# A fifth pair of column blocks in partial sums, a sixth slot for exponentials, and new order tables, in a two-layer attention and token-mixing kernel

## The chip, the core and the metric

The kernel runs on one core of a Trainium2 chip. The metric is the device time of one execution in microseconds. Lower is better. A core has a matrix engine (PE, which the kernel calls tensor), a vector engine (DVE, vector), an activation engine (ACT, scalar), a general engine (POOL, gpsimd) and an engine that issues transfers (SP, sync). Each works through its own list of instructions in order, and they wait for one another through semaphores.

## The reference

Two layers, each an attention half and a token-mixing half. S = 2048 tokens, D = 512, 32 heads of 16, a causal window of W = 256, F = 1792. All inputs are bf16.

```python
def _A_ref(x, wqkv, wo):
    qkv = (x @ wqkv).reshape(B, S, 3, H, Dh).transpose(2, 0, 3, 1, 4)
    q, k, v = qkv[0], qkv[1], qkv[2]
    scores = einsum("bhqd,bhkd->bhqk", q, k) * Dh ** -0.5
    mask = (i - j >= 0) & (i - j < 256)
    p = softmax(where(mask, scores, -1e9))
    o = einsum("bhqk,bhkd->bhqd", p, v)
    return o.transpose(0, 2, 1, 3).reshape(B, S, D) @ wo

def _B_ref(x, w1, b1, w2, b2):
    h = layernorm(x)
    u = gelu(einsum("bsd,sf->bdf", h, w1) + b1)
    return (einsum("bdf,fs->bds", u, w2) + b2).transpose(0, 2, 1)

x = A_x
x = x + _A_ref(layernorm(x), wqkv, wo)
x = x + _B_ref(layernorm(x), w1, b1, w2, b2)
x = x + _A_ref(layernorm(x), wqkv, wo)
x = x + _B_ref(layernorm(x), w1, b1, w2, b2)
```

The second half mixes over tokens: its first product sums over all 2048 tokens, so a value of u needs the normalised input x-hat (`xh_sb`) of every token.

## The kernel before

**How the order comes about.** The program is written as jobs that record operations with what they read and write. A list of jobs is sorted by due time and then visited in the order of a table, `ORDER`. A second table, `BANKS`, gives the PSUM bank (6 or 7) of the helper products. A third, `LINES`, gives the list of each of the five engines outright: which operation stands at which place, and for copies, masks and normalisations that more than one engine can do, on which of them it stands. These tables are packed strings. The semaphores follow from the recorded reads and writes. All large transfers are issued by SP, so a transfer that waits holds back those behind it in SP's list.

**Attention.** Each layer works on 4 groups Q of 512 queries, 4 head tiles t of 8 heads, and 9 steps m, so 144 steps. A step has scores on PE (L795, in cells of 64x64, into one of two halves of four PSUM banks), an exponential on ACT (L806, into slot n % NSLOT of `p_sb`), a mask on DVE or POOL (L823), and PV on PE (L844, banks 4 and 5). After m = 8 the sums are copied out to `oU` and `o2` (L440 on DVE, L442 on ACT, which are the two ends of one helper, `copy_out`), and transfers collect denominators (den_c<-oU) and the rest (oU<-o). Between the steps PE does the projections of q (L591), k (L622) and v (L695), transposes (L567, L580), the normalise product (L887) and the product with wo (L760). The layer norm has statistics (L525, L526) on DVE and small operations on POOL, and is applied (xh_sb) on ACT (L547), or by DVE or POOL (L544). L637 is ACT's half of masking k and q, L632 DVE's; L710 and L715 write `v_all`.

**Partial sums.** The 14 blocks of 128 columns of w1 are handled in 7 pairs. For the first PART = 8 blocks, `job_part` sums over chunks 0 to 7 (tokens 0 to 1023) while attention still works on the later tokens. It reads the lower weights from `w1low`, which holds two pairs, and uses 64 matmuls of 64x64 cells for a pair (L607). The sums go to `ubuf` as fp32 (`acc_at`).

**The MLP.** `job_u` computes u block by block, the whole blocks first, then the part blocks. A whole block has four groups of 4 matmuls of 128x128 by 128x512 (L983), a part block has the last two groups, and DVE adds the partial sum (L988). ACT applies gelu (L990). The upper weights of the part pairs lie in `xhT` (pairs 0 and 1) and `k_sb` (pairs 2 and 3), the weights of the three whole pairs in the three slices of `w1buf`; the third slice is loaded once for both layers. `job_y` multiplies by w2 (L1029). w2's homes are `w1buf[0]`, `w1buf[1]` and the two halves of `oU`. In layer 0 the tiles 8 to 15 of y are computed inside layer 1's attention, in cells (L607 too); the last tile of layer 1 is done in halves (L1017). The sum with the residual is on DVE (L1033, L1006, L1021).

**Hand-overs.** There are three. From attention to the MLP: after the last PV come the normalise product, wo, two layer norms, and x-hat of tokens 1536 to 2047 (tiles 12 to 15), and PE fills the time with u groups that need only the earlier tiles. From layer 0 to layer 1: after the first eight tiles of y come the layer norm of the first tokens, transposes, and k, q and v of the first group. Inside attention: every second head tile ends with the copies and transfers named above.

Of the kernel before, what the change touches and what calls it, by code (L numbers as in the profile page):

```python
# [10 lines left out]
P = 128  # L11
# [5 lines left out]
PART = 8  # L17
# [12 lines left out]
def _table(*text):  # L30
# [5 lines left out]
    'c-pm-Ne;ju3<DYe|It<36QUtoiNu9qWIOQ~ckvvCUEkdu!hhkTGe1YTP~@rQU0fFp^)x;4x-$AF=Njp%un%%{$-(R<s119<{N!Zp&wOBPJZ2gw'  # L36
    '_#DUKdY*TM)IMraJ>OSnL0d(ACotVqnr}=Y&BW*Olgl)%J+933^`8{tWL?s+0Cx')
ORDER = _table(
    'c-jTQ17Hvc00q#G>{_;$ZQEM5ZQHnPo6ELs+qP}qdjKJXM+g|95E5aK5^)h0kr5i<5E0Q40Z|YM(U1_a5EU^I196Z5fry9Lh>v7Qj6}$YBuIgz'
    'NQ2}^g|x_l)JTU+$d86dkF3ao?8uB_$c1dkgPh2K0OUh%6ht}XMPU>`Q4~TE)I~{@MsZX{36w=CR74q+M<wh-5UQXlDx*58p%yxzChDLDx}gGU'  # L40
    'qdpp=I~t%KnxPR|U?TdWC7Pf$nxidRp$*!jGlrlO+My%5peuS}9@e8bMxh7#qZbCD9|mGHrei1uU^up+4+di-{=*22#TbmoZVbZ&Ou;xD!emUt'
    'RLsO|%)%VZ#SARKB+SPmEJQGt;sh3BIhJ81R^cqxVhuK6HP&GXHen;SVg){9Gqzv{wqqB*;4=1OC-&k14&pwJ;4qHiDQ@5tj^YeX;yCu;JWk^r'
    'F5(jI;R3EAB(LBauHz4G;}-7VChp=P9^eVy;5i=S5uV{CUg0&~;sqk{15)!nKH?odAt}G(D}Lh}e&Hv`4EzBw1pgrnO))gXGXk?R3L`T*OEQ45'
    '7@N^pkx?0!aTt*aS%V1}pNW}_F&K`Cn1m@9ipiOZe-X%(OvAKH$Mg)#{EWve%*f2l#9WNY?99fT%)=ba&AiOVRxHQ@EW*NU$YLDDLM+PSEWu7J'
    '%~CAOaxB9N3}Sg!VI|gLW!7X}R%dNCU>(+DBQ|DzR%J6bXHzy|OSWKJwr3l5VLNtaNA_TEc4K$;Vm}UGPj+Qr4&p!#<zNnDAO6RYoX9a8!PXqd'
    '(HzV1oWRMP!v37eX`IU0oWWU~$N8MZxm?60T*$>-%3!YGYA)wWuHrhb<$7-CHE!TlZsc_i;R5dAGG5^(?&frE;Z5G=X0G8a-rx>y<xXznF7D+%'
    'p5y`U=P4fMSsv$69^?fc;|ZST5uW2Ap5aBF=Oy0ZWj^LzKHz;m;ypg(dp_fHzTi`S<P*N+8@}Z$zUDiA;3t0JAAaR`M$<Qb<}ZfV4~EcB{w4K~'
    'zZpjs6iQM^g;p3vRX9adVue*?MNlN=RSX3vtD-2n;wh$LDYfD%ff6acnkcCfD!Gy<nF3W#sZ>)Ll}<&JM(LGZnbl93ludb*LpfDnxm8g4)k#y8'
    'PlZ)L#Z*W=)LNxgROMAll~h(0RasS3O+yr0HB?o#Rb91IR}EE1jnzQS)JRR$LM@d`DV0H4lveH3M$HwZR_dU(YOgZttZwR}3hJto>aG&%rM~K|'
    '0qUc{>aRf>rjDwo5gMxD8m)mErLh{L@tUC7nxtu3pk<n<8JeP5>Z$3PsX3afd77`)TC9aSpkOW4a;?xv?b0f()EceTIIY(@ZPX@h&=zghHf`52'  # L50
    '?a)r`(QfV4WbM--ZPh^?)(IWaQ61N5oz!`q(J5WjSzXX2UDge~*A?B>65Y{l-PAK(*EQYO13l7H-O@RQ@I$@OW4+Z?J<)T$)JMJ1Ywgz;z0(JM'
    ')=z!XJ^j`Xebq1h(>KBLEB#eS({^ZwaeRkzIEQsaf7c&HaU@4@fFnDaqdTUPI)-CAj^jDJqdJx2I*}7Ni4!`pW4Vk2oy;kn+&P`W>73eWT*zIW'
    '!kL`jX`R&>oyB!r#krls&79r2T*P^t*L_^rrCiL#o!R+a!j)Xs*__YiT+!7X<kGI}f-dTkuIXy7=kl)M`mXDSZsaCz>I!b*R&L|gZtsq6;M#8M'
    '4sPx)uIldY?4IuC9`5DdZs*4C?|vTW0dDCb9_GOw>7gFs;U4309__In?+Kpd$?ofEp5m#V=^38o*<R!W-tRfy>p@=XQQqfep6iL8=fghe`JV1W'
    'KH?=_=mlQvV6XCKZ}Cbm_X=<IHt+NvZ}cXw_Xe-=TCesluk#LX_imr`d7tqmAN4U`^>Lr_37_^2pYuhZ^=)79Jzw!P-}hx-_Z{E#1K;&6KlCF%'
    '_7ndP&4=a!')
LINES = {
    "tensor": _table(
    'c-jrshkFRt769;j?>Xn5dv22ojaH4KjVDIZMA1GJv4a>-(HfPg5yYO!vqzMo)>C_ab`ce|pAa>kM6H_PqgIOw5<!T({t>_LS5bwkN~*G|qN=Je'
    '6|O#35h_wORne-Nicu|8JJnjXQD3M&DnTWw8ETZ8ppw;EHD66p^VA}>O6^e#)i$+KZB!f7Nwq^AP+QecYM(l!Zm1*bjC!JutBdM_%2J|ltE=iy'  # L60
    'bxWO4)72yOhssrD^-J}a%2A|Wr~=hk7uE0TNL@+?>Eb#>m((BXP+duf>)tv{SJ$8DT6&`Xr;gI|bzR+3ch?JaU)@5->4Ey9UaNcQ;W|kV(8F}1'
    '9;=gesve^!>uGw9UZ!(&1+z+T)JODEy;7&>4SJhCs_*EZ^?qI5?9gd?pFXHFb%s8p>zVWVy6$GK>EHED{fB<2|J2#~vCh|5^h;f+-)J_@3^0Kv'
    'zyzDpCdrgH<xHpvF<`2iDkjndnJg1wJ~cH>9dq4uG__3=)7f+}TTCzWjp=Lln?+`*8EN{MA;!QsGs28DlgwnZ*~~Gs&3yA8^TaGOOU+8N!E}IB'
    'v%~B$8Rn4LZPLs!bKIOXr%W+8Z_b&E=8|awcg=cuWbT*;Cf~$Cp?P5}6c~a)cpC=6`%nVPL0JfeN^lgyAq?umC8z-npgDMmg2vDaVxS#7Gyj4w'
    ';VbA0U&Azrg#OSQ5+EMNKnRS0p^yZfa3Una1egNJU~v}Agt>4ZR=^xs4y$1el)z1}5q7~r*aBN29kxLVWWshh1Bc-!$bt+w4OihN?0{6b2RGmj'
    'JcPgCH59;8$bnn{RQL>nFb{(9ITXRt_zsrB7Z8Fkp%Q+Cp%{U+u`JfZy4VaGVhaqzcGwXUFb+Fl0QSUK?1Ayv2NN*~Be5EOg4J;<j>8&Q6F<ez'
    'a0ZUWWc&_i<2)RQOK=dbz{R*62jdzXf~#>e4#i=Zg2QnWZo>n(AJgy=9>NiL7;`We8{q=X#&tLmJ)On^e1mUMCceOzn1$ysA8+7AEW{!dK#%bm'
    '22oK`^aS(p6_%zl6iUHVj*3xn3ZxQLiK<c<g-``5Pw!I%MbhWghU!uSYDm%4oZ8Y58cP4B(G*90DS^6EFN&vuG>XR40GdD}X(p|u*|dPNXg;l='
# [274 lines left out]
def bass_interleave_layers__sliding_block__mixer_token_mlp__prompt_kernel(  # L343
# [816 lines left out]
```

## Time and profile before

| | |
|---|---|
| three runs | 504.71, 505.14, 503.58 us (median 504.71) |
| the profiled execution | 504.01 us |
| its span on the core | 502.3 us |
| TensorE clock granted | 0.999 |

The profiled execution's own time is 1.7 us more than its span. The profile page has the busy time of each engine over the span, the chain of work that ended last, and groups of instructions by line. The windows cut the span into stages and give each engine's busy time there. Roughly, layer 0's attention runs from 14 to 164 us, the hand-over to its MLP from 164 to 188, the MLP from there to 230, layer 1's attention from about 232 to 408, and its MLP from there to the end. Three rows of each list of waits give the scale of what the engines waited for (engine, result and line that waited, what it waited for, total, times, longest):

```profile
ACT xh_sb L547 <- POOL shift L541: 34.7, 5, 11.5
...
ACT ubuf L990 <- DVE ps L988: 13.0, 14, 2.0
...
PE ps L591 <- issue: 2.7, 17, 0.2
PE ps L795 <- ACT p_sb L806: 2.3, 6, 0.7
...
PE ps L695 <- ACT wqkv L686: 1.1, 1, 1.1
```

ACT has long waits, since it is little used outside attention. PE's waits are few and short.

### The profile page before, as it was taken

The numbers are of one execution on the slowest core, as the hardware profiler recorded it, in microseconds if no ns is written. First come the engines' busy times: TensorE is split into PE (matmuls) and PEld (weight loads), VectorE is DVE, ScalarE is ACT, GpSimd is POOL, SyncE is SP. The second block draws the span as 40 slices with busy tenths as digits, with TensorE's granted clock in tenths as the row PEclk, the third lists the DMA queues.
The fourth block names the chain that finished last, engine by engine and source line by source line (L and its number), as shares of the span: only waits on it lengthen the run. The fifth ranks groups of instructions, "written<-read, shape, count | busy, mean of one in ns | idle before, by whom it ended". The sixth has DMA issues, their size and how long they took to land.

```text
span 502.3 us, 19381 instructions
## 1 busy us (share of the span) xinstructions
PE 474.3 (94%) x8385; PEld 272.0 (54%) x8454; DVE 323.4 (64%) x660; ACT 315.6 (63%) x381; POOL 213.1 (42%) x375
## 2 busy tenths in 40 slices
PE   8898989998999999998998999999999999999997
PEld 4454556555766444444444776566547754444444
DVE  7989988887663571366897447878886549131222
ACT  2898999997999314400776669889989960340000
POOL 5897756664564030001874555577544312200000
PEclk9999999999999999999999999999999999999999
DMA  6922222242222725050002140114214256050661
GB/s 209 96 79 84 70 71 77 85 114 68 78 62 70 216 79 147 0 147 1 24 9 61 50 137 15 38 61 136 85 47 114 71 156 185 0 146 12 198 200 52
DMA packets 76516, 44.52 MB, mean 89 GB/s; under 512 B 8976, under 2 KB 75408, under 8 KB 76432
## 3 DMA queue, kind: packets, MB, share of 16 engines
q1 hardware_dynamic: 72560, 43.27, 29.3%
q0 software_dynamic: 3872, 0.02, 1.4%
q8 instruction: 66, 1.08, 0.9%
q14 instruction: 18, 0.15, 0.1%
HBM read 32.51 MB, written 2.10 MB: 69 GB/s over the span
## 4 chain that ended last, share of the span: by engine, by line
PE 70%; ACT 8%; DVE 6%; POOL 6%; issue 4%; DMA 3%; SPq 2%; DVEq 0%; ACTq 0%; POOLq 0%
PE ps L1029 14%; PE ps L983 13%; PE ps L795 9%; PE ps L844 8%; ACT p_sb L806 7%; PE ps L591 7%; PE ps L607 7%; PE ps L760 4%; PE ps L695 4%; POOL p_sb L823 3%; SPq L434 2%; PE ps L519 1%; PE ps L887 1%; DMA w1buf<-in_B_w_dram 1%; POOL xh_sb L544 1%
## 5 line engine op out<-in xcount | busy, mean ns | idle before, releaser
L806 ACT ACTIVATE p_sb<-ps 128x1024 bf16<-128x1024 f32 (+8 forms) x288 | 261.5, 977 | 47.4 <-PE ps L795 39.0
L823 POOL TENSOR_TENSOR p_sb<-p_sb,edge 128x128 bf16<-128x128 bf16 (+2 forms) x263 | 127.4, 491 | 114.1 <-ACT p_sb L806 99.3
L795 PE MATMUL ps<-q_sb,k_sb 64*64 64x288 bf16 (+8 forms) x2816 | 108.5, 249 | 3.4 <-ACT p_sb L806 2.3
L844 PE MATMUL ps<-p_sb,v_all 64*34 64x288 bf16 (+17 forms) x2816 | 92.1, 246 | 4.4 <-issue 1.5
L795 PEld LDWEIGHTS ps<-q_sb,k_sb 64*64 64x64 bf16 x2816 | 60.0, 106 | 46.6 <-ACT p_sb L806 22.6
L844 PEld LDWEIGHTS ps<-p_sb,v_all 64*64 64x64 bf16 (+1 forms) x2816 | 60.0, 100 | 21.5 <-POOL p_sb L823 6.3
L591 PE MATMUL ps<-xhT,wqkv 128*128 128x512 bf16 x214 | 55.4, 380 | 4.8 <-issue 2.7
L823 DVE TENSOR_TENSOR p_sb<-p_sb,edge 128x128 bf16<-128x128 bf16 (+2 forms) x137 | 39.9, 300 | 21.9 <-ACT p_sb L806 14.5
L1033 DVE SCALAR_TENSOR_TENSOR x_sb<-ps,b2col,x_sb 128x512 bf16<-128x512 f32 x23 | 17.1, 750 | 44.4 <-PE ps L1029 43.9
L537 POOL TENSOR_TENSOR rstd<-vare,mhalf 128x4 f32<-128x4 f32 (+1 forms) x17 | 16.6, 977 | 67.1 <-DVE vare L535 53.9
L983 PE MATMUL ps<-xh_sb,w1buf 128*128 128x512 bf16 x186 | 44.1, 379 | 0.6 <-issue 0.5
L525 DVE BATCH_NORM_STATS2 stats<-x_sb 128x6 f32<-128x512 bf16 x64 | 43.0, 681 | 0.6
L710 POOL TENSOR_TENSOR v_all<-vt,even 128x1024 bf16<-128x1024 f32 (+2 forms) x23 | 34.3, 1495 | 17.3 <-DVE vt L698 17.3
L547 ACT ACTIVATE xh_sb<-x_sb,shift,rstd 128x512 bf16<-128x512 bf16 x11 | 8.8, 813 | 50.5 <-POOL shift L541 34.7
L632 DVE TENSOR_TENSOR k_sb<-ps,half 128x1024 bf16<-128x1024 f32 (+1 forms) x32 | 37.3, 1166 | 4.7 <-PE ps L622 2.4
L1029 PE MATMUL ps<-ubuf,w1buf 128*128 128x512 bf16 x165 | 37.4, 379 | 0.2
L607 PE MATMUL ps<-xh_sb,w1low 64*64 64x512 bf16 x512 | 35.5, 377 | 0.1
L1029 PE MATMUL ps<-ubuf,oU 128*128 128x512 bf16 x150 | 34.5, 379 | 0.2
L988 DVE TENSOR_TENSOR ps<-ps,ubuf 128x512 f32<-128x512 f32 x16 | 11.2, 700 | 35.1 <-PE ps L983 35.1
L591 PEld LDWEIGHTS ps<-xhT,wqkv 128*128 128x128 bf16 x240 | 19.5, 98 | 26.5 <-issue 4.4
L695 PE MATMUL ps<-xhT,wqkv 128*128 128x512 bf16 x114 | 30.1, 380 | 3.5 <-issue 1.4
L990 ACT ACTIVATE ubuf<-ps,b1col 128x512 bf16<-128x512 f32 x28 | 19.0, 686 | 22.9 <-DVE ps L988 13.0
(89 smaller groups left out, 531.4 us busy)
## 6 DMA issues: line engine op xcount, KB each, us to landing
w1buf<-in_B_w_dram SPq DMA_DIRECT2D x30, 256.0 KB
w1buf<-in_B_w_dram SPq DMA_DIRECT2D x50, 128.0 KB
oU<-in_B_w_dram SPq DMA_DIRECT2D x18, 256.0 KB
oU<-o SPq DMA_DIRECT2D x16, 256.0 KB
w1low<-in_B_w_dram SPq DMA_DIRECT2D x32, 128.0 KB
q_sb<-qt SPq DMA_DIRECT2D x120, 32.0 KB
xhT<-in_B_w_dram SPq DMA_DIRECT2D x4, 512.0 KB
k_sb<-in_B_w_dram SPq DMA_DIRECT2D x4, 512.0 KB
```

Source lines behind the costliest of these rows:

```text
L525: dve(lambda e: e.bn_stats(stats[:, t, :], x_sb[:, t, :]), 690, prio, reads=[R("x", t)], writes=[R("stats", t)])
L591: last = e.matmul(ps[:, b, :], lhsT=wqkv[:, c, c0:c0 + P], rhs=xhT[:, buf, c, :], start=(c == 0), stop=(c == 3))
L607: last = e.matmul(ps[64 * h:64 * h + 64, banks[r ^ swap], :], lhsT=lhs(r ^ swap, c, rows, 64 * h), rhs=rhs(r ^ swap, c, rows), start=(c == ...
L632: return e.tensor_tensor(dst, src.unsqueeze(2).to_broadcast([P, n, 2, w]), mask[:].unsqueeze(1).unsqueeze(3).to_broadcast([P, n, 2, w]), o ...
L695: last = e.matmul(ps[:, b, :], lhsT=wv[:, c], rhs=xhT[:, buf, c, :], start=(c == 0), stop=(c == 3))
L710: return e.tensor_tensor(dst, src.unsqueeze(2).to_broadcast([P, n, 2, DH]), even[:].unsqueeze(1).unsqueeze(3).to_broadcast([P, n, 2, DH]), ...
L795: last = e.matmul(ps[64 * c:64 * c + 64, 2 * half + r, 32 * i0:32 * i1], lhsT=k_sb[rows, ring, t, kb % 16, :], rhs=q_sb[rows, t, c, 32 * i ...
L806: exps[plan.job] = last_exp[0] = plan.op({ACT: (170 + int(2 * (512 - c0) * 0.84), lambda e: e.activation(p_sb[:, slot, :, c0:512], ps[:, 2 ...
L823: return e.tensor_tensor(v, v, g, op=ALU.mult)
L844: last = e.matmul(ps[64 * r:64 * r + w, B_O + (c ^ r), 32 * i0:32 * i1], lhsT=v_all[rows, pos - 32 * c:pos - 32 * c + w], rhs=p_sb[rows, s ...
L983: r = e.matmul(ps[:, b, :], lhsT=blk[:, sc - 8 * part, (ft % 2) * P:(ft % 2 + 1) * P], rhs=xh_sb[:, sc, :], start=(sc == 8 * part), stop=( ...
L1029: r = e.matmul(ps[:, b, :], lhsT=blk[:, turn[n], (st % 2) * P:(st % 2 + 1) * P], rhs=u_at(turn[n]), start=(n == 0), stop=(n == NFT - 1))
```

## The change

PART goes from 8 to 10, so job_part handles five pairs. The third slice of w1buf goes, and an own buffer `w1more` of half its size holds the upper weights of the fifth pair; ubuf grows by two blocks. p_sb has six slots. The due time of the fifth pair's upper load is 60 us into the layer. All three tables are new, so places and engines of many operations are new too, also where nothing else changed.

```diff
@@ -14,7 +14,7 @@
-PART = 8
+PART = 10
@@ -33,91 +33,92 @@
 BANKS = _table(
...
 ORDER = _table(
...
 LINES = {
...
@@ -361,7 +362,7 @@
-    NSLOT = 5
+    NSLOT = 6
@@ -387,7 +388,8 @@
-        w1buf = sb("w1buf", [P, 3, NT, 256])
+        w1buf = sb("w1buf", [P, 2, NT, 256])
+        w1more = sb("w1more", [P, 8, 256])
         w1low = sb("w1low", [P, 2, 8, 256])
         ubuf = sb("ubuf", [P, (NFT + PART) * D])
@@ -927,6 +929,8 @@
             if fb >= NLOW:
                 return w1buf[:, fb - NLOW], [R("w1", fb - NLOW, j) for j in range(8)]
+            if fb == 4:
+                return w1more[:], [R("w1more")]
@@ -1095,7 +1099,7 @@
-                todo.append((base + (76 + 2.5 * k if k < 2 else 100 + 0.1 * k), lambda p, k=k: w1_high_dma(k, p)))
+                todo.append((base + (76 + 2.5 * k if k < 2 else 100 + 0.1 * k if k < 4 else 60), lambda p, k=k: w1_high_dma(k, p)))
```

What the tables change can be counted in the lists of the two programs, operations by engine:

| operation | before | after |
|---|---|---|
| PE L607, cells | 960 | 1088 |
| PE L983, u groups | 320 | 288 |
| DVE L988, adds of partial sums | 16 | 20 |
| ACT copies to o, oU, qt, ubuf | 6, 7, 9, 5 | 9, 8, 10, 6 |
| ACT copies of 128x1024 to xhT | 1 | 3 |
| ACT masks to k_sb, to q_sb | 2, 0 | 4, 2 |
| ACT to v_all, 128x512 | 4 | 2 |
| x-hat on ACT, DVE, POOL | 11, 28, 25 | 12, 32, 20 |
| SP loads to w1buf (w1), w1low, w1more | 50, 32, 0 | 42, 40, 2 |

Of the order three things are named by the prediction. In front of k of layer 1 (L622) there stood 4 matmuls of y after the last transposes, and now there stand 14. The 64 cells matmuls of the fifth pair stand, in both layers, behind the last PV and ahead of the first normalise product. Where layer 0's third query group ends its first pair of head tiles, SP's list held eight transfers from the first of the denominators to oU<-o, and now holds six.

More of the change, by code (lines that the diff above doesn't have):

```diff
@@ L40 @@
[L40 to L44, printed above, removed]
@@ new lines @@
+    ')w*i;r>k&{uEEv0Cig${-bza'),
+    "scalar": _table(
+    'c-jTQYfKho6ae6Jd(V5$`-4@Au|g}<yktwAE*!WTbJMl3BFkp7NiO+8mQ5)gk?4jj$xT?0I`P7~IHqOF`qTv$iB3(oD9kcPsf|Wi>4q*e*7Mv4'
+    'g-`%bz<ely8puEk?11G^1?yoGG(jD-!Zz3sZSW0rLOb+87hHsH7=ZI|3Vwq@_!|_5;BFj-yKp?_;$(aTXJP@qk40FFkK<CTz!mrgc4HN;#X4-n'
+    '9axX8*oL2B20L&ceuZbT7yIxs4&XJsg)b41Qx=V;QItoM=wX^p`81nepi(NQ3R*=!(`u@rT56<bYN0*UPKW4AIzeZshtAOz`h#xLZ6Z#b&G+&+'
+    'p2YcF$kTWZ&*LY#gcoudFXLDEHD1Y8yp}=gxSqH0cK(15a|fT`(|nFE@UPs@H~BwKk|m>LjEt3;GE0i2SW2W+%4C_WmI|qsTG=QKvQ=7Sw;Ys8'
@@ new lines @@
+    'IV9b3NlwdN>5`-JkBkht!NQD?6FA%-ri6bbKMc#bFfmLGvqD*@3~z_#us!SwABJrq6Apxi@I^QlPKGn#`*0zg55I@2;d;o@937!!b&O8bsamK-'
+    'I#-|8=k!%wrE9cWYqVZlb*t{tPxPQ>v{O%Nul}gNXun?7>v}^uj*b)JJ#kumC^qVQnjeee+&H99#l>+!TpG*c`nVx(jGJRq+!@>B-gqQ_9=qc4'
+    'csBOLzIZtf#KDNBmSx#?r{&rMHr|$4fz7aw;uM=_#rCW%wsKo;Z`xb-u5Gq0)?&NuW7}sL>#+TH%8uJH`_6u_KD%PqY|u)5gb&*R&+{CA(5L&O'
+    'KHKN`0$=3i?q1<5y~=C6(VKmzxA`-E#6R_~z0-g4Uhnrye#8IrKYhrD{f?BK^3r4JTc40D<)-=R`Lrfgr<c=`RGD5(@1&;mda6z9QbXF5{s;A3'
+    '$m9'),
+    "gpsimd": _table(
```

142 lines of the change are left out of this document (69 added, 73 removed).

## The prediction

> **What bounds the kernel now.** I read busy times and chain shares first, then the windows by stage, then the waits of TensorE and ScalarE, then chain and timeline where a wait is longer than 0.5 us. Busy times and the shares of the chain that ended last:
>
> ```profile
> PE 474.3 (94%) x8385; PEld 272.0 (54%) x8454; DVE 323.4 (64%) x660; ACT 315.6 (63%) x381; POOL 213.1 (42%) x375
> PE 70%; ACT 8%; DVE 6%; POOL 6%; issue 4%; DMA 3%; SPq 2%; DVEq 0%; ACTq 0%; POOLq 0%
> ```
>
> PE is busy 474.3 of 502.3 us. An edit that leaves its work alone can gain at most the 28 us in which it stands idle. The windows say where those are (columns: stretch, length, busy time of each engine, clock, DMA share, GB/s):
>
> ```profile
> 60.00:112.00 52.00, 48.37 (x1276) 29.92 (x1279) 44.34 (x86) 49.64 (x56) 29.68 (x45) 1.00 0.30 86
> 112.00:164.00 52.00, 48.65 (x1415) 33.15 (x1422) 30.59 (x63) 47.83 (x53) 27.03 (x50) 1.00 0.25 72
> 164.00:188.00 24.00, 23.40 (x183) 10.96 (x186) 16.58 (x36) 5.20 (x9) 4.72 (x8) 1.00 0.51 149
> 188.00:230.00 42.00, 41.79 (x199) 19.16 (x201) 16.56 (x31) 12.74 (x19) 3.69 (x6) 1.00 0.30 88
> 230.00:260.00 30.00, 26.82 (x381) 14.14 (x385) 25.07 (x50) 16.35 (x22) 16.27 (x27) 1.00 0.05 12
> 352.00:408.00 56.00, 53.79 (x1420) 35.96 (x1428) 38.54 (x72) 51.57 (x59) 24.24 (x45) 1.00 0.31 88
> ```
>
> In the MLP (188 to 230) PE idles 0.2 us of 42: only fewer matmuls would help there. In layer 0's attention (60 to 164) PE has 97.0 of 104 us and ACT 97.5: two engines are full at once, ACT with 6.5 us to spare. The hand-over to layer 1 (230 to 260) has PE's largest gap, 3.2 us. What ACT and PE waited for (total, times, longest):
>
> ```profile
> ACT p_sb L806 <- PE ps L795: 39.0, 47, 11.6
> ...
> ACT p_sb L806 <- PE ps L844: 5.5, 8, 1.7
> ...
> PE ps L622 <- DVE xhT L440: 1.8, 1, 1.8
> ...
> PE ps L844 <- DVE o L440: 0.9, 1, 0.9
> ```
>
> The exponentials mostly wait for scores, little for a slot that a PV matmul (L844) frees. PE's two named stalls are single events: k of layer 1, and a PV behind a copy.
>
> **The fifth pair.** The chain prices both kinds of matmul (start, us, line, count):
>
> ```profile
> 151.63 1.73 PE ps L607 x32
> ...
> 183.31 7.77 PE ps L983 x36
> ```
>
> 32 of L607 take 1.73 us (54 ns each, in 64x64 cells), 36 of L983 7.77 (216 ns). The change moves the lower half (chunks 0 to 7) of two column blocks from job_u, 2 x 8 = 16 of L983 per layer (320 to 288 in all), 3.45 us, to job_part, 64 of L607 per layer (960 to 1088), 3.46 us: PE's work is unchanged. Nor does it move to where ACT could cover it. In the changed PE list the 64 stand in both layers behind the last PV, just ahead of the first normalise (L887), where PE is alone and full (164 to 188: 23.4 of 24); only 8 more L607 stand inside an attention, 0.43 us, given back after it. Value 0; if the list ran as an own stage with nothing beside it, it is still 0. What comes with the pair: two DVE adds per layer (L988, 16 to 20, 0.70 each) under PE groups of 0.86 us; uncovered they cost 4 x 0.70 = 2.8, a loss only. Two copies to ubuf per layer (0.59) beside the outproj and normalise matmuls. Four more low-weight loads per layer on SP (w1low 32 to 40) and one of w1more, against eight w1buf loads fewer; the pair's low weights come when the third pair's are read, its upper ones behind the fourth query group's first exponential, a quarter of the attention ahead of the MLP that reads them; eight w2 loads of twice the size took 8.2 us, so four cost about 2 us if nothing hid them, and behind them on SP stand q and oU loads. I take 0: the DMA share in attention is 0.25 to 0.31.
>
> **Hand-over to layer 1.** In front of k (L622) DVE's copies of the transposes come late:
>
> ```profile
> 231.94 0.39 DVE L440 COPY xhT<-ps 128x512 bf16<-128x512 bf16 x1
> ...
> 232.39 1.05 PE L622 MATMUL ps<-xhT,wqkv 128*128 128x256 bf16 x8 [1.84 <-DVE xhT L440]
> ```
>
> Before, one group of y (four L1029, 0.86 us) stands between the last transposes and k. The new list puts 14 L1029 there (14 x 0.216 = 3.0 us), work that had to be done anyway. The 1.84 us stall is covered by 2.2 us more: -1.6, keeping 0.2 for copies shifted by the new order. Bounds -1.84 and 0 (if DVE's copies come later by as much).
>
> **The output copy in layer 0.** At 116 to 122 the den_c and oU loads queue on SP, and PE (0.94) and ACT (0.80, 0.91, 0.92 in its timeline) stall behind them:
>
> ```profile
> 116.77 1.96 DMA den_c<-oU
> ...
> 118.75 2.35 DMA oU<-o
> ```
>
> Before, SP's list holds eight loads from the first denominator to oU<-o, one of which (w1buf) waits for an exponential; the new list holds six, with no such wait among them. Value -0.9, PE's stall; bounds 0 and -2.6 (ACT's three gaps).
>
> **Copies on ACT.** The new lists give ACT, in both attentions, 3 more copies to o (0.61 each), 1 to oU (0.63), 1 of qt (0.60), 1 to ubuf (0.59), 2 large ones to xhT (1.05), and 2 fewer to v_all (0.72): 1.8 + 0.6 + 0.6 + 0.6 + 2.1 - 1.4 = 4.3 us, some 3.6 of it in layer 0. Every one stands ahead of exponentials in ACT's queue, and scores wait for the banks that these free. The chain passes through exponentials for 10.2% of 60 to 112 and 17.3% of 112 to 164, so I take 0.15 x 4.3 = +0.6. Bounds 0 (the spare 6.5 us take them) and +4.3. DVE is relieved by the same copies; it is not full in any of these windows except 60 to 112 (44.3 of 52).
>
> The Trainium skill (ScalarE: Activation LUTs, section What ACT_TABLE_LOAD costs) says that back-to-back activations overlap by about 93 ns. By it each of the six net added copies costs 0.09 less, 0.5 in all, and this term would be 0.15 x 3.8 = +0.6 too. The trace agrees: five exponentials of 1.03 us each took 4.75 us, 0.10 of overlap apiece.
>
> **Six slots.** An exponential may run one step further ahead of the PV that frees its slot. At most this gives back the 5.5 us that ACT waited on L844. But 5.2 of them lie at 240 to 408, where PE is busy 160.1 of 168 us: ACT would wait for PE elsewhere. I take the same 0.15, -0.8; bounds 0 and -5.5.
>
> **Start.** The first v projection (L695) waited 1.1 us on an ACT copy of wqkv; in the new lists it does not, but the first exponential comes only about 0.2 earlier: -0.2, bounds -1.1 and 0.
>
> **From attention to the MLP.** The tiles 12 to 15 of the last group need outproj, LN twice and x-hat before the u groups that read them:
>
> ```profile
> 187.41 1.52 ACT L547 ACTIVATE xh_sb<-x_sb,shift,rstd 128x512 bf16<-128x512 bf16 x2 [8.22 <-POOL shift L541]
> ```
>
> x-hat is done at 188.93; PE reaches the first reader after 7 groups of 0.86 from 183.31, at 189.3. With one more pair in parts only 6 such groups are left in both layers, so PE comes 0.86 earlier; x-hat comes about 0.5 earlier, as two of its four applies go to DVE (two in 1.05 us, against 1.52 on ACT). The margin of 0.4 (in layer 1 x-hat at 431.4, PE at 431.8: the same) goes to about 0. I take 0.2 per layer, as the LN chain may not bring all of the 0.5: +0.4; bounds 0 and +1.7 (one group per layer). The w2 loads behind it took 8.2 us in a burst and have 8 to 12 us before their first reader: 0.
>
> **Sum.** -1.6 - 0.9 + 0.6 - 0.8 - 0.2 + 0.4 = -2.5. The profiled run took 504.01 us, 502.28 of them span; so 501.5 for such a run. The median of the runs shown is 0.7 higher, 504.71, and so 502.2.
>
> **Rivals.**
> 1. Slower: ACT sets the pace of layer 0's attention. The copies count in full, +4.3, and as ACT is then always behind, neither the SP stretch nor the sixth slot gives anything: 504.7 + 4.3 - 1.6 - 0.2 + 0.4 = 507.6. It decides from where some 70% of the 4.3 lie on the path. For it: ACT is busy 97.5 of 104 us. Against: the 6.5 us spare, and ACT's 39 us of waiting on scores. Chance 0.20.
> 2. The hand-over runs dry: normalise and LN finish 1.3 us later per layer, since the pair's copies and stats share DVE with them (adds and stats now stand ahead of the reciprocal in layer 1). 502.2 + 2.6 = 504.8. For it: a margin of 0.4 at 189. Against: PE's pair there, 3.5 us, is cover itself. Chance 0.10.
> 3. Removed waits are taken over by others, the change being a re-sorting of equal work: 504.2 to 504.7. For it: PE 93% and ACT 94% full at once, so what one stall gives the next may take. Against: the stall at 232 has pure PE work behind it. Chance 0.17.
> 4. The pair is hidden after all, PE running closer: 3.45 - 0.43 = 3.0 us per layer off on top of the sum, 502.2 - 6.0 = 496.2. Against: the list puts it where PE is alone and full (23.4 of 24). Chance 0.03. The Trainium skill (Trainium Kernel Development and Optimization, section Performance Expectations) holds that busy matmul time tells little of the distance to the roofline, because matmuls are pipelined, and takes the weight loads' share instead. Here that is 54%, and by this rule PE would have room for rival 4. The rows of the MLP speak against it: 36 matmuls follow one another at 0.216 us with no gap while PEld is at 46%.
>
> **How the numbers follow.** The forecast has 0.50, its own range 499.5 to 503.9: most bounds of the gains on one side, the loss of either large gain on the other. The range reaches to 499.0 and, into rival 1, 507.2. This kernel's measurement can tell about 0.3%, 1.5 us: faster is under 503.2, slower over 506.2. Faster: 0.42 from the forecast, 0.01 each from rivals 2 and 3, 0.03 from 4: 0.47. Same: 0.08 + 0.03 + 0.06 + 0.13 = 0.30. Slower: 0.17 from rival 1, 0.03 each from 2 and 3: 0.23.
>
> **What would show it.** Right: no wait of L622 on xhT over 0.3 us at 232; no PE stall on o near 121; ACT's waits on L844 under 4 us; L607 at 54 ns per instruction in its new place; PE without a gap over 0.3 at the first L983 that reads tile 12. Wrong: ACT over 100 us busy in the first 104 us of full attention with that stage longer (rival 1), a new wait of PE on x-hat or on oT at the MLP's start (rival 2), equal stages with other names among the waits (rival 3).

## The result and the profile after

The changed kernel takes 496.98 us (median of 4 runs, 496.20 to 497.66), the kernel before beside it 504.92 (503.58 to 506.26). The ratio is 0.9842, 95% interval 0.9809 to 0.9875: 7.9 us faster. The forecast was 2.5 us; 496.98 lies below its range. The profiled run took 497.66 us with a span of 495.9 (before 504.01 and 502.3), so the two traces have 6.4 us to explain.

The page of the changed kernel, busy times and the shares of the chain that ended last:

```profile
PE 472.4 (95%) x8478; PEld 272.3 (55%) x8550; DVE 325.5 (66%) x661; ACT 320.6 (65%) x392; POOL 211.4 (43%) x372
PE 78%; DVE 9%; ACT 5%; issue 4%; DMA 2%; SPq 2%; POOL 1%; DVEq 0%; ACTq 0%; POOLq 0%
```

PE has about as much to do as before (474.3) in a shorter span. The chain has moved from ACT (8 to 5%) and POOL (6 to 1%) to PE (70 to 78%) and DVE (6 to 9%). Where the time left is read from the starts of PE's matmuls in the traces, in us; the last column is a second profile of the changed kernel:

| stage | before | changed | changed again |
|---|---|---|---|
| start to the first scores | 14.76 | 15.26 | 13.93 |
| layer 0, first scores to last PV | 150.86 | 148.99 | 149.20 |
| last PV to the first y | 42.71 | 42.33 | 42.34 |
| first y to the first transpose of layer 1 | 20.29 | 20.28 | 20.28 |
| that transpose to the first scores | 10.37 | 8.43 | 8.43 |
| layer 1, first scores to last PV | 169.04 | 165.95 | 165.41 |
| last PV to the first y | 42.74 | 43.12 | 43.14 |

From the first y of layer 1 to the end all three take 51.5. The start differs by 1.3 us between two runs of one kernel, so nothing of it is put down to the change. What remains is three pieces: layer 0's attention 1.7 to 1.9, the way to layer 1's scores 1.9, layer 1's attention 3.1 to 3.6. The split is good to about 1 us: the kernel with the filler in the old lists (below), the same as before in layer 0, shows 149.68 there, and the one with another SP order in layer 0 shows 170.19 in layer 1. The hand-overs to the MLP cancel. Much of the gain lies early in each attention: the first 56 exponentials take 54.7 and 55.3 us in layer 0 (before 56.4), and 65.1 and 64.0 in layer 1 (before 67.4). The windows of the changed kernel (stretch, length, busy time and count of PE, PEld, DVE, ACT, POOL, clock, DMA share, GB/s):

```profile
60.00:112.00 52.00, 48.40 (x1315) 30.59 (x1326) 44.47 (x83) 50.44 (x57) 31.23 (x48) 1.00 0.26 74
112.00:164.00 52.00, 49.17 (x1368) 33.18 (x1370) 30.92 (x59) 48.26 (x54) 28.61 (x54) 1.00 0.30 88
164.00:188.00 24.00, 23.50 (x232) 10.65 (x224) 16.84 (x38) 4.28 (x7) 4.65 (x7) 1.00 0.48 138
188.00:230.00 42.00, 41.79 (x200) 19.03 (x203) 19.08 (x37) 11.48 (x17) 2.11 (x3) 1.00 0.30 88
230.00:260.00 30.00, 29.25 (x438) 16.16 (x444) 27.26 (x52) 22.65 (x34) 16.76 (x33) 1.00 0.08 22
```

ACT is busier than before in the two windows of layer 0's attention (98.7 of 104 us, was 97.5) and the stage is shorter all the same. PE's gap at 230 to 260 has shrunk from 3.2 to 0.75 us. The waits (total, times, longest):

```profile
ACT p_sb L808 <- PE ps L797: 24.8, 41, 2.2
...
ACT p_sb L808 <- PE ps L846: 1.5, 5, 0.4
```

```profile
PE ps L797 <- ACT p_sb L808: 4.3, 7, 1.2
...
PE ps L697 <- ACT wqkv L688: 1.0, 1, 1.0
```

ACT's waits for a slot went from 5.5 to 1.5 us, its waits for scores from 39.0 to 24.8. In exchange PE now waits 4.3 us (2.3 before) for an exponential to free a score bank, and the v projection still waits 1.0 us for wqkv. The timeline of PE at the start of layer 1 in the changed kernel (start, us, operation, count, and in brackets an idle time ahead of it):

```profile
228.61 2.11 PE L1033 MATMUL ps<-ubuf,oU 128*128 128x512 bf16 x9
230.55 0.39 PE L569 MATMUL ps<-ident,xh_sb 128*128 128x128 bf16 x4
230.78 1.03 PE L1033 MATMUL ps<-ubuf,oU 128*128 128x512 bf16 x4
231.64 1.91 PE L624 MATMUL ps<-xhT,wqkv 128*128 128x256 bf16 x16
```

Where PE stood 1.84 us ahead of k, y matmuls now run among and behind the transposes, and k follows without a gap. Between the first transpose and the first scores stand 18 y matmuls, as before the change: then 4 of them stood among the transposes, none behind the last, and 14 between the halves of k and q. Now all 18 stand ahead of k.

### The profile page after: what moved, and what is told of

The parts are those of the page before. It is cut to its first block, busy times and chain, and to the rows that moved or that the text cites. A ratio compares the mean times of both kernels' runs of the same rounds, so it can differ in the third digit from the quotient of the medians.

```text
span 495.9 us, 19594 instructions
## 1 busy us (share of the span) xinstructions
PE 472.4 (95%) x8478; PEld 272.3 (55%) x8550; DVE 325.5 (66%) x661; ACT 320.6 (65%) x392; POOL 211.4 (43%) x372
## 4 chain that ended last, share of the span: by engine, by line
PE 78%; DVE 9%; ACT 5%; issue 4%; DMA 2%; SPq 2%; POOL 1%; DVEq 0%; ACTq 0%; POOLq 0%
PE ps L1033 14%; PE ps L987 13%; PE ps L609 12%; PE ps L797 10%; PE ps L846 9%; PE ps L593 7%; PE ps L762 5%; ACT p_sb L808 4%; PE ps L697 4%; PE ps L521 2%; SPq L436 2%; PE ps L889 1%; DMA oU<-o 1%; DVE p_sb L825 1%; DVE vt L700 1%
## 5 line engine op out<-in xcount | busy, mean ns | idle before, releaser
L808 ACT ACTIVATE p_sb<-ps 128x1024 bf16<-128x1024 f32 (+8 forms) x288 | 261.4, 975 | 28.7 <-PE ps L797 24.8
L825 POOL TENSOR_TENSOR p_sb<-p_sb,edge 128x256 bf16<-128x256 bf16 (+2 forms) x266 | 131.2, 499 | 111.7 <-ACT p_sb L808 97.8
L846 PE MATMUL ps<-p_sb,v_all 64*34 64x288 bf16 (+17 forms) x2816 | 89.1, 245 | 1.8 <-DVE p_sb L825 0.8
L846 PEld LDWEIGHTS ps<-p_sb,v_all 64*34 64x34 bf16 (+1 forms) x2816 | 60.6, 100 | 12.1 <-issue 3.6
L593 PE MATMUL ps<-xhT,wqkv 128*128 128x512 bf16 x212 | 55.3, 380 | 4.1 <-issue 3.0
L825 DVE TENSOR_TENSOR p_sb<-p_sb,edge 128x128 bf16<-128x128 bf16 (+2 forms) x134 | 35.5, 279 | 20.3 <-ACT p_sb L808 18.0
L1037 DVE SCALAR_TENSOR_TENSOR x_sb<-ps,b2col,x_sb 128x512 bf16<-128x512 f32 x23 | 17.0, 748 | 43.3 <-PE ps L1033 42.7
L527 DVE BATCH_NORM_STATS2 stats<-x_sb 128x6 f32<-128x512 bf16 x64 | 42.7, 681 | 0.6
L609 PE MATMUL ps<-xh_sb,w1low 64*64 64x512 bf16 x640 | 41.7, 377 | 0.1
L712 POOL TENSOR_TENSOR v_all<-vt,even 128x1024 bf16<-128x1024 f32 (+2 forms) x22 | 33.0, 1504 | 5.0 <-DVE vt L700 2.7
L593 PEld LDWEIGHTS ps<-xhT,wqkv 128*128 128x128 bf16 x240 | 19.4, 98 | 24.8 <-issue 4.2
L992 DVE TENSOR_TENSOR ps<-ps,ubuf 128x512 f32<-128x512 f32 x20 | 14.0, 699 | 26.5 <-PE ps L987 26.4
L762 PE MATMUL ps<-wo_sb,oT 128*128 128x512 bf16 x117 | 29.4, 380 | 1.7 <-issue 0.8
```

What stands on the lines that cost most here:

```text
L527: dve(lambda e: e.bn_stats(stats[:, t, :], x_sb[:, t, :]), 690, prio, reads=[R("x", t)], writes=[R("stats", t)])
L593: last = e.matmul(ps[:, b, :], lhsT=wqkv[:, c, c0:c0 + P], rhs=xhT[:, buf, c, :], start=(c == 0), stop=(c == 3))
L609: last = e.matmul(ps[64 * h:64 * h + 64, banks[r ^ swap], :], lhsT=lhs(r ^ swap, c, rows, 64 * h), rhs=rhs(r ^ swap, c, rows), start=(c == ...
L762: last = e.matmul(ps[:, b, :], lhsT=oT[:, buf, t, i * P:(i + 1) * P], rhs=wo_sb[:, t, :], start=(t == 0), stop=(t == 3))
L808: exps[plan.job] = last_exp[0] = plan.op({ACT: (170 + int(2 * (512 - c0) * 0.84), lambda e: e.activation(p_sb[:, slot, :, c0:512], ps[:, 2 ...
L825: return e.tensor_tensor(v, v, g, op=ALU.mult)
```

## The experiments

Most of them edit the order tables of one of the two kernels. An entry names the engine and place it is taken from and those where it is put; operations, weights and data stay the same:

```diff
+MOVES = [('tensor', 478, 'tensor', 477), ...]
+for _a, _i, _b, _j in MOVES:
+    LINES[_b].insert(_j, LINES[_a].pop(_i))
```

Below, "new lists" are those of the changed kernel and "old lists" those of the kernel before. Line numbers shift by up to 20 with what an edit adds. The runs came in groups, each with the kernel before beside it, so kernels of different groups are compared by their ratios to it.

### The filler ahead of layer 1's k

**Taken back out of the new lists.** The 14 matmuls of one y tile go behind the first halves of k and q, where the old list has 14.

```diff
+MOVES = [('tensor', 478, 'tensor', 477), ('tensor', 480, 'tensor', 478),
+         ('tensor', 482, 'tensor', 479), ('tensor', 482, 'tensor', 481)]
```

> The changed kernel with 14 matmuls of y (tile 4) put back behind the first halves of k and q of layer 1, so that between the last transpose and k nothing stands, as in the kernel before. Theory F (the 1.95 us gained between the transposes and the first scores of layer 1 are this filler): 1.6 to 1.95 us slower, 498.6 to 499.0, and a wait of k on a copy to xhT of about 1.8 us. Theory H (they come from the k and q masks that now stand on ACT beside DVE): under 0.5 us slower.

Measured: 500.87 us, ratio 0.9903 [0.9875, 0.9931] to the kernel before, so 3.1 to 3.7 us slower than the changed kernel by its two ratios (0.9842 here, 0.9830 in a later group). From the first transpose to the first scores it took 12.14 us, 3.7 more than the changed kernel. PE's waits in this kernel between 225 and 240:

```profile
PE ps L629 <- DVE xhT L447: 1.8, 1, 1.8
PE ps L629 <- DVE x_sb L1042: 0.8, 1, 0.8
PE ps L574 <- DVE xhT L447: 0.4, 1, 0.4
```

The 1.8 us stall of k on the copy of the transposes is back, just as before the change. Another 1.2 are waits on DVE, probably because its list, with the y add (L1042), was laid out for the new place; some 0.7 of the 3.7 are in no wait of these rows. The masks of k and q stay on ACT in this kernel, so they are not what the gain came from. The gain in this place is the filler's.

**Put into the old lists.** The 14 y matmuls between the halves of k and q go in front of k, 10 between the last two transposes and 4 behind them.

```diff
+MOVES = [('tensor', 476, 'tensor', 473), ('tensor', 478, 'tensor', 475)]
```

> The kernel before with the 14 matmuls of y's tile 7 put ahead of k of layer 1 (10 between the last two transposes, 4 behind the last) in place of between its halves. Nothing else changes. If the stall at 232 is only a lack of filler: 1.6 to 1.9 us faster than before, and PE's wait of k on xhT gone. If k, q and their masks are the longer chain from there on: under 0.7 us.

Measured: 504.29 against 504.60, ratio 1.0001 [0.9986, 1.0015]. PE's timeline shows k in one run at the place where it had waited 1.84 us:

```profile
232.00 1.91 PE L627 MATMUL ps<-xhT,wqkv 128*128 128x256 bf16 x16
```

Transposes to first scores fell from 10.37 to 8.61 us, by 1.76. But layer 1's attention grew from 169.04 to 171.20 us in the profiled run, and the total stayed in the median of 11 runs. So an early start of layer 1 is only kept if the attention behind it keeps it. Where it was lost is not shown: 1.2 of the 2.2 us are one stop of PE without a named cause (last section), and the kernel with another SP order has 170.19 in layer 1 without any edit there.

### Six slots

**Five slots in the new lists.** With five, 69 steps of the program order and five places of the lists must move so that no PV stands behind the exponential that needs its slot. A second kernel has the same moves with all six slots.

```diff
-    NSLOT = 6
+    NSLOT = 5
+ORDER_MOVES = [(25, 24), (32, 29), (39, 37), ...]
+MOVES = [('gpsimd', 49, 'gpsimd', 48), ('scalar', 28, 'scalar', 27), ('tensor', 59, 'tensor', 58),
+         ('tensor', 60, 'tensor', 59), ('tensor', 796, 'tensor', 795)]
```

> The changed kernel with five slots for exponentials in place of six; 69 PV steps move ahead in program order (by up to 6 jobs) and five operations move one place in the engines' lists, so that five slots suffice. Theory S (the sixth slot is what made both attentions shorter): the 3.1 us of layer 1's attention and most of the 1.9 of layer 0's come back, 501 to 502 us, and ACT's waits on PV matmuls go from 1.5 us back to about 5.5. Theory O (the gain lies in the order and the engines chosen, the slot is worth the 0.8 us that was forecast): 497.5 to 498.

> The control of the run with five slots: the changed kernel with the same 69 PV steps earlier in program order and the same five list moves, but with six slots. If the 18.6 us of that run were the slot alone: 497 us as the changed kernel, and ACT's waits on PV back at 1.5 us (from 35.7). If the moves cost part of it: over 499.

Measured: 515.59 us with five slots, ratio 1.021 [1.0161, 1.0258]; 495.82 with the moves alone, 0.982 [0.9794, 0.9845]. The moves cost nothing, the slot 19.7 us by the two ratios, far more than either theory had. ACT's waits with five slots, then with the moves alone:

```profile
ACT p_sb L817 <- PE ps L855: 35.7, 40, 4.0
ACT p_sb L817 <- PE ps L806: 15.3, 28, 2.1
```

```profile
ACT p_sb L817 <- PE ps L806: 23.5, 39, 2.2
...
ACT p_sb L817 <- PE ps L855: 1.5, 5, 0.4
```

In the new lists an exponential stands one score further ahead of the PV that frees its slot. Without the slot it waits there 40 times, and scores wait for exponentials in turn (14.4 us, 4.3 with the slot).

**Six slots in the old lists.** The sixth lies in a part of w1low that is idle then, and serves the first 60 exponentials of each layer.

```diff
+    EARLY6 = 60
+        def slot_of(n):
+            return n % 6 if n < EARLY6 else n % NSLOT
+        def p_at(slot):
+            return p_sb[:, slot] if slot < NSLOT else w1low[:, 1, 4:8].rearrange(...)
```

> The kernel before, lists unchanged, with a sixth slot for the exponentials of the first 60 steps of each layer, in the part of w1low that is free then. Theory S (waiting for a slot costs time in the kernel before): ACT's waits on PV matmuls go from 5.5 to about 1 us and 1 to 3 us are gained in layer 1's attention. Theory O (the slot is worth nothing until the lists send the scores further ahead of PV): under 0.5 us.

Measured: 504.75 against 504.60, ratio 1.0007 [0.9990, 1.0024]. ACT's waits:

```profile
ACT p_sb L817 <- PE ps L806: 40.7, 49, 11.6
...
ACT w1low L817 <- PE ps L806: 3.0, 5, 0.9
...
ACT p_sb L817 <- PE ps L855: 0.7, 1, 0.7
```

The 5.5 us of waits for a slot are all but gone and nothing is gained: ACT waits for scores instead. The exponentials that write the sixth slot have a row of their own (w1low), so the waits for scores went from 39.0 to 43.7, 4.7 more, and those for a slot down by 4.8.

### Copies on ACT

**Back to DVE in the new lists.** The table of the change shows the net count. Behind it stand 15 copies out of PSUM (4 to o, 5 to oU, 4 of qt, 2 large ones to xhT) and one write of v_all that went from DVE to ACT, and others that went the other way. These 16 go back.

```diff
+MOVES = [['scalar', 356, 'vector', 591], ['scalar', 325, 'vector', 556], ...,
+         ['scalar', 29, 'vector', 70], ['scalar', 24, 'vector', 65]]
```

> The changed kernel with 16 PSUM copies of the two attentions (9 to oU and o, 4 of qt, 2 to xhT, 1 to v_all), which the kernel before had on DVE, moved from ACT's list back to DVE's, at the place that has the same time in the trace. ACT loses 16 x 0.62 = 10 us of work. Theory A (copies on ACT cost time, 0.15 of their length as forecast): 1.5 us faster, 495.5. Theory D (they relieve DVE, which then masks and copies sooner, and this is where the attentions' gain came from): 2 to 5 us slower, 499 to 502.

Measured: 502.68 us, ratio 0.9939 [0.9914, 0.9965]: 4.9 to 5.5 us slower than the changed kernel by its two ratios. Layer 0's attention took 151.93 us and layer 1's 167.75 (changed 149.0 to 149.2 and 165.4 to 166.0); transposes to scores stayed at 8.43. Windows of this kernel, then of the changed one and the one before for the first stretch:

```profile
14.00:60.00 46.00, 41.22 (x796) 22.72 (x808) 43.71 (x100) 37.71 (x51) 36.60 (x67) 1.00 0.43 80
60.00:112.00 52.00, 47.92 (x1230) 29.49 (x1244) 45.30 (x87) 48.57 (x54) 29.91 (x47) 1.00 0.26 77
```

```profile
14.00:60.00 46.00, 42.64 (x821) 23.61 (x835) 42.91 (x101) 42.48 (x60) 37.01 (x69) 1.00 0.42 85
```

```profile
14.00:60.00 46.00, 42.57 (x801) 23.37 (x814) 42.09 (x94) 40.24 (x56) 39.05 (x73) 1.00 0.44 84
```

From 14 to 60 DVE was the fuller of the two before the change, 42.09 of 46 us against ACT's 40.24. With the copies back, DVE has 43.71 and ACT 37.71. (PE's busy time says nothing here: 42.64 and 44.69 in two profiles of the changed kernel.) The first 56 exponentials of layer 0 take 56.8 us, against 54.7 and 55.3 in the changed kernel, and the chain that ended last in them goes through DVE for some 42%:

```profile
by line: ACT p_sb L813 9.3%; DVE stats L532 8.4%; DVE k_sb L639 8.0%; PE ps L802 7.8%; PE ps L851 7.0%; DVE xh_sb L551 6.4%; PE ps L598 6.0%; DVE p_sb L830 5.7%; DVE vt L705 5.2%; DVE xhT L447 4.0%; DVE v_all L717 4.0%; issue 3.3%; PE ps L7
```

In the changed kernel's row (shown further down) the DVE entries that can be seen sum to some 17%. So in the new lists DVE has to be relieved in this stretch, and ACT has the room. In layer 1 the first 56 exponentials hardly depend on the copies (65.3 us); what is lost there lies behind them.

**To ACT in the old lists.** The same 16.

```diff
+MOVES = [('vector', 65, 'scalar', 20), ('vector', 75, 'scalar', 29), ..., ('vector', 577, 'scalar', 361)]
```

> The kernel before with the same 16 PSUM copies, which the change puts on ACT, taken from DVE's list and put on ACT's at the place of the same time. Theory D (DVE, whose masks and copies stand ahead of PV, is the engine to relieve; the run with the copies back on DVE lost 5.7 us): 2 to 5 us faster. Theory P (they pay only in lists that are arranged for them; here they delay exponentials): 0 to 3 us slower.

Measured: 508.0 against 504.6, ratio 1.0079 [1.0054, 1.0103]: 3.4 us slower. In the profiles layer 0's attention grew from 150.86 to 152.82 us and layer 1's from 169.04 to 170.76. PE's waits:

```profile
PE ps L800 <- ACT p_sb L811: 3.5, 10, 0.7
...
PE ps L596 <- ACT qt L447: 1.2, 1, 1.2
```

Here the copies do what the first rival feared: scores (L800) wait for exponentials that stand behind them, 3.5 us (2.3 before), and a projection waits 1.2 us for a copy of qt. One edit is worth about 5 us in one order and costs 3.4 in the other.

### All three in the old lists, and a longer lead

Filler, copies and the sixth slot together:

> The kernel before with all three: the filler ahead of k, the 16 copies on ACT, six slots for the first 60 steps. If the parts add up and are what the change gains: 4 to 8 us faster, 497 to 501. If only the filler counts alone: 503.

Measured: 507.77, ratio 1.0069 [1.0047, 1.0091], 3.2 us slower than before. The parts together do not make the change.

One theory was that the new lists gain by running the scores one step further ahead throughout. In the old lists with six slots, each PV of steps 2 to 55 goes behind one more score (87 places of PE's list), without and with the 16 copies on ACT.

```diff
+ORDER_MOVES = [(655, 656), (653, 654), (646, 647), ...]
+MOVES = [('tensor', 667, 'tensor', 668), ('tensor', 658, 'tensor', 659), ...]
```

> The kernel before with six slots for the first 60 steps of each layer, and with PV one score later in PE's list (and in program order) for steps 2 to 55 of each layer, 87 places in all: the lead of the scores over PV that the sixth slot allows. Counted from exponential 0 to 56 and 144 to 200 (kernel before 56.4 and 67.4 us; five kernels with its lists 56.4 to 57.7 and 66.4 to 67.4; changed kernel 54.7 to 55.3 and 64.0 to 65.1). Theory L (the lead is what the slot buys): both stretches 1.5 to 2.5 us shorter, 501 to 502 us. Theory X (the lead pays only together with copies on ACT or other moves of the new lists): within 0.5 us in both.

> The same with the 16 copies on ACT (11 of them lie in the two stretches). Theory LC (the lead makes copies on ACT harmless and DVE's relief then counts): both stretches 1.5 to 2.5 us shorter than in the kernel before. Theory P (it lies in the single places of the new lists): both as long as in the kernel before or longer, as in the run with the copies alone (57.7 and 66.4).

Measured: 512.43, ratio 1.0145 [1.0094, 1.0196], and 515.45, ratio 1.0193 [1.0141, 1.0245]. PE's waits without the copies:

```profile
PE ps L864 <- DVE o L451: 3.2, 2, 1.9
PE ps L815 <- ACT p_sb L826: 3.0, 10, 0.5
```

A uniform lead makes it worse; that theory falls.

### The SP queue in layer 0

Three loads of the old SP list go behind the output's loads.

```diff
+MOVES = [('sync', 121, 'sync', 122), ('sync', 119, 'sync', 122), ('sync', 117, 'sync', 122)]
```

> The kernel before with three of SP's transfers (a w1buf, a w1low and a q_sb load) put behind oU<-o of layer 0's third group, first pair of head tiles. Theory Q (the stall at 116 to 122 was SP's queue, as forecast): 0.9 us faster than before, and PE's wait on the o copy gone. Theory W (oU<-o waits for its own chain of two transfers, SP's order hardly matters): under 0.3 us.

Measured: 504.91 against 505.42, ratio 0.9978 [0.9950, 1.0007]. No effect that could be told from none. PE's 0.9 us wait on the copy to o is gone from this place, and no transfer stands in the chain from 114 to 124 any more, so the queue was the cause of the stall. Yet layer 0's attention took 151.12 us, against 150.86: the time was not gained.

### The fifth pair

In the changed kernel chunks 2 to 7 of the fifth pair's lower products are computed for 32 of 512 columns, the rest of that part is left out.

```diff
+                        n = 32 if thin and c0 else 512
-                                    last = e.matmul(ps[64 * h:64 * h + 64, banks[r ^ swap], :], ...
+                                    last = e.matmul(ps[64 * h:64 * h + 64, banks[r ^ swap], 0:n], ...
```

> The changed kernel with three quarters of the fifth pair's lower products left out (chunks 2 to 7 are computed for 32 of 512 columns only), so that its 64 matmuls take about 1.1 us in place of 3.46; the instruction count stays. If the pair lies on PE's path as forecast: 2 x 2.4 = 4.7 us faster than the changed kernel, 492. If it is hidden in the hand-over (rival 4, and the changed time is near its number): under 1 us faster.

Measured: 496.31 us, ratio 0.9830 [0.9805, 0.9855]; the changed kernel beside it has 496.02. Windows of the hand-over in layer 0, thin pair and changed kernel (second profile):

```profile
162.00:186.00 24.00, 21.34 (x248) 9.97 (x247) 17.01 (x38) 4.92 (x8) 4.91 (x10) 1.00 0.54 155
```

```profile
162.00:186.00 24.00, 23.93 (x250) 10.83 (x248) 17.69 (x39) 5.13 (x8) 5.30 (x9) 1.00 0.51 151
```

PE has 2.6 us less to do there and nothing is gained. In the changed kernel (second profile) the chain of this stretch is PE's work alone:

```profile
by line: PE ps L987 60.6%; PE ps L762 19.9%; PE ps L609 14.1%; PE ps L889 4.2%; PE ps L846 1.7%; issue 0.2%
```

In the thin kernel the chain (start, us, what) goes over the transfers:

```profile
166.22 1.89 DMA den_c<-oU
...
168.18 5.79 DMA oU<-o
...
173.99 1.29 DVE oT L898 x2
...
175.33 0.64 PE ps L891 x32
```

Here the transfers of denominators and output, and the normalise behind them, set the end of the stage. This transfer of the output was late, though: in the second profile of the changed kernel the same one, issued at 167.59, had landed by 172.46, after 4.9 us at most. The work left out turns into 2.5 us of waiting, 1.2 of it for DVE's copy of the pair's own sums, which frees the banks, 0.8 for x-hat and 0.5 for the normalised output:

```profile
PE ps L891 <- DVE ubuf L443: 1.2, 1, 1.2
PE ps L989 <- ACT xh_sb L550: 0.8, 1, 0.8
PE ps L891 <- DVE oT L898: 0.5, 1, 0.5
```

In layer 1 it is the same copy:

```profile
PE ps L891 <- DVE ubuf L443: 1.7, 1, 1.7
```

The second profile of the changed kernel lists no wait of PE in either stretch. So PE's work, the copies on DVE and the transfers are about equally long there, and PE's work alone can be cut without gain.

### The start, and the changed kernel again

One of PE's warm-up products goes behind the first two transposes, one of the first two x-hat tiles goes from ACT to DVE, and ACT's copies of wqkv go ahead of its k mask.

```diff
+MOVES = [('tensor', 11, 'tensor', 13), ('scalar', 5, 'scalar', 9), ('scalar', 5, 'scalar', 8), ('scalar', 1, 'vector', 25)]
```

> The changed kernel with its start rearranged: one of PE's warm-up products behind the first two transposes (as in the kernel before), one of the first two x-hat tiles on DVE beside ACT, and ACT's copies of wqkv ahead of its k mask. The first scores stand at 15.26 us in the changed kernel, 14.76 in the kernel before, with a wait of v on wqkv of 1.0. If these three are the start's chain: first scores 0.7 to 1.2 us earlier and the whole 0.7 to 1.2 faster. If the loads of x or wqkv set the start: under 0.3.

> The changed kernel itself, on the same chip as the other three, as their reference: 497.0 us; the first scores at 15.3.

Measured: 496.16, ratio 0.9825 [0.9802, 0.9849], and 496.02, ratio 0.9830 [0.9805, 0.9854]. The first scores came at 14.43 us with the edit, and at 15.26 and 13.93 in two profiles without it. Inconclusive, since the start of the same kernel moves more than that. The two profiles differ in PE's warm-up products, the first rows of PE (first and second profile):

```profile
1.70 8.15 PE L521 MATMUL ps<-ident 128*128 128x512 bf16 x24 [1.70 <-POOL ident L465]
```

```profile
1.71 6.81 PE L521 MATMUL ps<-ident 128*128 128x512 bf16 x24 [1.71 <-POOL ident L465]
```

By their starts in the traces, the first 13 of the 24 came about 0.43 us apart in the first profile and the rest 0.22, in the second only the first 7; the transposes begin right behind them, at 9.69 and 8.44 us.

No kernel of the study is measurably faster than the changed one; 495.82 and 496.16 equal its 496.02.

## Why the prediction was wrong

The forecast had the sign and one large term right and the size of the attentions wrong. By its steps:

- **Hand-over to layer 1, -1.6.** Right: -1.94 in the profile, and the stall of 1.8 comes back when the filler is taken out. The place was misread: before, no y matmul stood behind the last transposes (the 4 named there stood among them), and of the 14 of the new list 10 stand between the last two transposes and 4 behind. That this term reached the total is part of the new order: the same filler in the old lists gained nothing.
- **Copies on ACT, +0.6. This is the step that failed**, in its sign. In the new lists the 16 copies on ACT are worth 4.9 to 5.5 us of gain. It failed at two choices. It took a net count, which hid 16 copies the one way and others the other. And it looked for room at 60 to 164 only, where ACT was the fuller engine; at 14 to 60 DVE was. The chain by line for the first 56 exponentials of layer 0, before and changed, shows who set the pace there:

```profile
by line: POOL p_sb L823 19.0%; ACT p_sb L806 13.8%; PE ps L795 11.8%; PE ps L591 10.7%; PE ps L844 8.9%; POOL v_all L710 6.6%; issue 6.5%; PE ps L695 6.4%; POOL xh_sb L544 2.7%; DVE vt L698 2.4%; PE ps L760 2.0%; DVE xh_sb L544 1.9%; POOL r
```

```profile
by line: ACT p_sb L808 17.4%; PE ps L797 12.9%; PE ps L593 12.5%; PE ps L846 9.3%; PE ps L697 6.7%; issue 5.3%; DVE p_sb L825 4.6%; DVE stats L527 4.3%; DVE k_sb L634 4.2%; POOL p_sb L825 3.7%; DVE vt L700 3.6%; PE ps L582 3.3%; PE ps L762 
```

  The masks on POOL and its v_all went from 25.6% of that path to 3.7% and below what the row shows; exponentials rose from 13.8 to 17.4%. So POOL, which the prediction gave no term, led before the change, and DVE takes over when the copies go back to it (some 42%).
- **Six slots, -0.8, and the factor 0.15.** The same mistake from the other side. A chain share of the old order was taken as the price of a microsecond in the new one, and the 5.5 us of old waits as the most a slot can be worth. The waits were worth 0 in the old lists, where waits for scores took their place, and the slot 19.7 us in the new ones. Both are true: the new order is laid out for the slot, as it is for the copies.
- **The output copy in layer 0, -0.9.** PE's 0.9 us stall on the copy to o went as said: 0.2 us, on ACT's copy, are left at this place (the 0.3 that PE still waits on o lie in layer 1). But the value was wrong in the old lists: with three loads moved the stall was gone there too, and no gain could be told from none (interval 2.5 us gained to 0.4 lost). What it is worth in the new lists stays open.
- **The three terms of the attentions together** were -1.1. Measured: -1.7 to -1.9 in layer 0, -3.1 to -3.6 in layer 1, so some 4 us more than forecast. This is most of the miss; layer 1, where nearly all of the slot's 0.8 and a small share of the copies were expected, gave the larger half.
- **The fifth pair, 0.** The number holds. Of the reason given, that PE is alone and full there, "full" holds and "alone" does not: with 2.6 us of PE's work left out nothing is gained, since the copies on DVE and the transfers end as late. The pair's 64 products took 1.88 and 1.92 us, a half each, in the second profile's chain: 59 to 60 ns an instruction in place of 54. The Trainium skill (Trainium Kernel Development and Optimization, section Performance Expectations) calls matmul busy time a bad metric for how close a kernel is to the roofline. The row agrees that it is no price: PE busy 23.93 of 24 us, and less work gains nothing; here the reason is the other paths. The prediction quoted that rule for the hidden pair and set it aside with rows of the MLP, not of the hand-over.
- **From attention to the MLP, +0.4.** Measured -0.4 in layer 0 and +0.4 in layer 1: nothing in sum.
- **Start, -0.2.** The wait on wqkv, said to go, is there with 1.0 us (0.6 in the second profile). Its price is below what the warm-up products change from run to run.
- **Rivals.** ACT as the pace (507.6) falls: ACT went above 98 us of 104 and the stage got shorter. It does hold for the old lists, where the copies cost 3.4. Removed waits taken over by others (504.2 to 504.7) holds for single parts in the old lists, filler, slot and SP order, and not for the change. The hidden pair (496.2) named nearly the right time by luck: its 3.0 us a layer would have to show between the last PV and the first y, and that stretch went from 42.7 to 42.3 and from 42.7 to 43.1 us. The hand-over running dry did not happen; the margin is about nil, as the thin pair shows.
- **The signs.** Four of the five signs of being right came: no wait of k on xhT, 0.2 us on o at its place, 1.5 us of waits for a slot, no gap of PE over 0.3 at the MLP. Only the 54 ns did not. They came although the size was wrong, because they speak of waits, and the sum of the removed waits was not the gain.

What stays open: which places of the new lists carry the attentions' gain. It is not any of the three parts alone, not the three put into the old lists, and not a lead of one score throughout. That the order as a whole, planned for the slot and the copies, carries it is what remains after these, and not itself shown. One candidate has no run: the new lists take work off POOL, with 20 x-hat tiles in place of 25, and 37.01 us busy from 14 to 60 in place of 39.05, and POOL led the path there before.

## What to carry to other kernels

When a change brings a new order with it, don't price its resources by the old trace's waits: a resource that the new order is laid out for can be worth several times the waits it removes from the old one (19.7 us against 5.5), or nothing without it. Look for the fullest engine stage by stage, the first stage too, before calling a moved operation a cost. A full engine in a hand-over may have other paths of the same length beside it: leave some of its work out and see whether the time moves.

## What was not expected of the hardware

Two profiles of one kernel reached their first scores at 13.93 and 15.26 us, because 24 warm-up products took 6.81 us in one and 8.15 in the other. The transfer oU<-o took 5.79 us in the hand-over of the thin kernel, beside a DMA share of 0.54, and 2.35 us in the middle of layer 0's attention in the kernel before. PE also stopped for 1.17 us inside a run of matmuls in layer 1's attention, with nothing in the profile to wait for, in the kernel with the filler in the old lists (its waits of PE):

```profile
PE ps L612 <- issue: 1.2, 1, 1.2
```

The other six edits of the old lists show a stop of 0.4 to 1.0 us at matmuls of the same line there, the kernel before none over 0.35. What PE waited for stays open.
